# An ALiBi sliding-window attention and mixture-of-experts kernel: all heads' P.V in split bf16, queries in permuted groups, a new order of work

## The chip, the cores and the metric

One core of one Trainium2 chip runs the kernel. The metric is the device time of one execution in microseconds (us).

## The reference

```python
# q, k, v: (8 batches, 8 heads, 576 tokens, 64), fp32
scores = scale * np.matmul(q, k.transpose(0, 1, 3, 2))
scores = np.where((rel >= 0) & (rel < 128), scores + bias, -1e9)   # rel = query - key, bias = -slope[head] * rel
attn = softmax(scores)
x = (attn @ v), heads side by side: 4608 tokens x 512
y_dense = relu(x @ w1_dense) @ w2_dense
e = argmax(x @ w_gate)          # one of 8 experts for each token
y = y_dense + softmax(x @ w_gate)[e] * (relu(x @ w1[e]) @ w2[e])   # all weights 512 x 512
```

## The kernel before

The attention works in 16 units `u`: one batch and four heads (`hq`). A unit loads k and q as one transfer each (`load_qk`), 18 tokens to a partition, 32 partitions to a head. DVE turns them in blocks of 32x32 (`turn`, L345), and ACT rounds them to fp32r while it puts the tokens back in order, with a step of 18 elements in its output (`round_qk`, L352). Unit 0's query is rounded by DVE.

Each unit then has two rounds `r` (key tiles 0, 1 and 2, 3, 4). TensorE (PE) adds mask and bias with small products (`add_masks`, L536) and the scores (`scores`, L556); ACT takes the exponential for two heads at a time, `p` = 0 or 1 (`exps`, L567). P is fp32 and its bf16 upper half is read in place. `lows` (L579, DVE) writes P minus that half into the lower half as bf16, and `prep_v` (L365, POOL) does the same to V. `attend` sums P.V in PSUM as three bf16 products (high.high, high.low, low.high; L623) for a pair of key and query tile. With `OPT["whole"]` of 1 and `whole_to` of 12, units 0 to 11 take the last of their four heads as one fp32 product instead (L604): that head then needs no low parts, so `lows` of p = 1 has 512 columns there in place of 1024 and `prep_v` three heads in place of four. The last key tile has 64 rows. `norm` divides by the sums, `flip` and `keep` transpose for the gate.

After each batch the gate's logits choose an expert, tokens get slots in a DRAM table by expert (`count`, `slots`), and POOL scatters the rows (`send`, L846). Expert work goes in 43 blocks of 128 rows of one expert: 11 blocks after batch 4, 9 after batch 6, and 23 late ones after batch 8. A block is fetched through the SP queue, DVE copies its expert weights (`bring`, L1034), PE does layer 1 (L1044) and layer 2 (L1056) for the expert and for the dense part, ACT the ReLU, DVE the sum (L1070), POOL the scatter to the output (L1074). Early blocks take the ReLU in two halves (L1384) and have one buffer `yo` for the sum; late ones take it as one instruction over two banks (L1319) and keep sums in the six `p` buffers.

All of it is issued in an order made ahead by `Plan.order`: every part has an engine, a cost, a wanted time (`PACE` by unit, an offset and step from `PLACE`) and rooms (buffers, `ROOMS`). A list scheduler picks, on each engine, the part with the least wanted time among those that can start within `SLACK` of the first. The chip then runs each engine's list in that order. `OPT["flat"]` of 1 makes the set `FLAT` empty, so the functions for flat loads aren't used.

## Time and profile before

| | |
|---|---|
| time, median of 3 | 434.71 us (429.52 to 437.95) |
| profiled execution | 433.74 us, span 431.8 us |
| mean granted clock of TensorE | 0.887 |
| busy, share of the span | PE 86%, DVE 59%, ACT 54%, POOL 48% |

The span is from the first to the last instruction; what remains of the execution's time lies around it. PE and PEld are TensorE's matmuls and weight loads, DVE VectorE, ACT ScalarE, POOL GpSimd, SP SyncE, whose queue issues most loads.

### The profile page before, as it was taken

The numbers are of one execution on the slowest core, as the hardware profiler recorded it, in microseconds if no ns is written. First come the engines' busy times: TensorE is split into PE (matmuls) and PEld (weight loads), VectorE is DVE, ScalarE is ACT, GpSimd is POOL, SyncE is SP. The second block draws the span as 40 slices with busy tenths as digits, with TensorE's granted clock in tenths as the row PEclk, the third lists the DMA queues.
The fourth block names the chain that finished last, engine by engine and source line by source line (L and its number), as shares of the span: only waits on it lengthen the run. The fifth ranks groups of instructions, "written<-read, shape, count | busy, mean of one in ns | idle before, by whom it ended". The sixth has DMA issues, their size and how long they took to land.

```text
span 431.8 us, 12406 instructions
## 1 busy us (share of the span) xinstructions
PE 370.2 (86%) x5005; PEld 285.7 (66%) x5039; DVE 252.9 (59%) x438; ACT 233.1 (54%) x274; POOL 206.6 (48%) x265
## 2 busy tenths in 40 slices
PE   3499989897897977999798999779876999999993
PEld 0377877685685865787666776667654676767681
DVE  5576736748597578458969898563532243434331
ACT  5656655624667747547638996324332444444442
POOL 5060450508687818637743447657362242424241
PEclk9999967958586995569979999979989999999998
DMA  9979777951969986995436722133263433434330
GB/s 212 261 176 218 148 156 174 161 151 57 225 173 189 268 186 180 137 249 150 113 81 179 196 52 75 46 73 107 74 181 88 111 89 96 79 97 110 91 99 13
DMA packets 88808, 59.60 MB, mean 138 GB/s; under 512 B 70959, under 2 KB 81199, under 8 KB 88752
## 3 DMA queue, kind: packets, MB, share of 16 engines
q1 hardware_dynamic: 73872, 34.54, 33.3%
q0 software_dynamic: 14736, 23.68, 24.2%
q8 instruction: 40, 0.66, 0.6%
q10 hardware_dynamic: 144, 0.59, 0.5%
q14 instruction: 16, 0.13, 0.1%
HBM read 47.29 MB, written 17.13 MB: 149 GB/s over the span
## 4 chain that ended last, share of the span: by engine, by line
PE 43%; issue 18%; DVE 15%; POOL 12%; DMA 6%; ACT 3%; POOLq 1%; DVEq 0%; SPq 0%; ACTq 0%
PE ax L623 12%; POOL out_dram L1074 7%; PE ax L604 7%; PE sq L556 6%; PE misc L1044 5%; PE misc L1056 4%; DVE p L579 4%; DVE stg L345 3%; PE misc L683 3%; PE sq L536 2%; DMA rawq<-in_q_dram 2%; PE misc L716 2%; DVE xf L642 2%; DVE ws L1034 2%; POOL xs_dram L846 2%
## 5 line engine op out<-in xcount | busy, mean ns | idle before, releaser
L623 PE MATMUL ax<-vf,p 128*128 128x65 bf16 (+5 forms) x1404 | 84.7, 212 | 20.1 <-DVE p L579 13.3
L623 PEld LDWEIGHTS <-p 128*128 128x128 bf16 (+2 forms) x1404 | 72.4, 113 | 35.2 <-DVE p L579 14.7
L579 DVE TENSOR_TENSOR p<-p 128x1024 bf16<-128x1024 f32 x64 | 77.5, 1241 | 10.8 <-ACT p L567 10.8
L567 ACT ACTIVATE p<-sq 128x1024 f32<-128x1024 f32 x64 | 63.0, 1024 | 36.5 <-PE sq L556 35.9
L846 POOL DMA_INDIRECT xs_dram<-xrow,slot x40 | 45.7, 1141 | 32.1 <-issue 12.5
L664 POOL CAST xrow<-xf 128x512 bf16<-128x512 f32 x32 | 27.9, 876 | 46.1 <-DVE xf L642 45.9
L1056 PE MATMUL misc<-w_all,hT 128*128 (+1 forms) x138 | 41.9, 399 | 8.2 <-DVE yo L1070 5.4
L1074 POOL DMA_INDIRECT out_dram<-p,xm x23 | 24.5, 1065 | 51.0 <-DVE p L1070 51.0
L352 ACT CAST kT<-stg 128x1152 fp32r<-128x1152 f32 x16 | 37.7, 2356 | 18.2 <-DVE stg L345 18.2
L604 PE MATMUL ax<-vf,p 128*128 128x65 f32 (+2 forms) x216 | 46.7, 343 | 0.0
L1384 ACT ACTIVATE hT<-misc 128x512 bf16<-128x512 f32 x40 | 24.2, 607 | 39.1 <-PE misc L1044 39.1
L1074 POOL DMA_INDIRECT out_dram<-yo,xm x20 | 24.2, 1208 | 43.6 <-DVE yo L1070 34.9
L1044 PEld LDWEIGHTS <-w_all 128*128 128x128 bf16 x688 | 40.4, 98 | 5.2 <-issue 3.3
L604 PEld LDWEIGHTS ax<-vf,p 128*128 128x128 f32 (+2 forms) x216 | 37.7, 241 | 1.9
L352 ACT CAST qT<-stg 128x1152 fp32r<-128x1152 f32 x15 | 35.4, 2359 | 3.6 <-DVE mx L753 2.4
L365 POOL TENSOR_TENSOR vf<-vf 128x960 bf16<-128x960 f32 (+1 forms) x15 | 29.6, 1971 | 14.5 <-DMA vf<-in_v_dram 14.4
L556 PE MATMUL sq<-qT,kT 32*128 32x256 f32 (+2 forms) x640 | 32.8, 344 | 4.2 <-DVE qT L352 3.6
L1319 ACT ACTIVATE xT<-sq 128x1024 bf16<-128x1024 f32 x23 | 23.5, 1023 | 23.8 <-PE sq L1044 23.8
L556 PEld LDWEIGHTS sq<-qT,kT 32*128 32x128 f32 (+1 forms) x640 | 26.9, 235 | 11.7 <-issue 5.6
L1070 DVE TENSOR_TENSOR yo<-misc,ye 128x512 f32<-128x512 f32 x20 | 13.8, 688 | 33.0 <-DMA out_dram<-yo,xm 25.4
L641 DVE RECIPROCAL recip<-ax 128x8 f32<-128x8 f32 x32 | 6.6, 207 | 43.9 <-PE ax L604 40.6
L1034 DVE COPY ws<-w_all 128x2048 bf16 x20 | 24.2, 1208 | 12.6 <-PE misc L1044 11.3
(127 smaller groups left out, 601.9 us busy)
## 6 DMA issues: line engine op xcount, KB each, us to landing
rawk<-in_k_dram SPq DMA_DIRECT2D x16, 576.0 KB
rawq<-in_q_dram SPq DMA_DIRECT2D x15, 576.0 KB
vf<-in_v_dram SPq DMA_DIRECT2D x64, 128.0 KB
w_all<-in_moe_w_dram POOLq DMA_DIRECT2D x16, 512.0 KB, 8.1
xs_dram<-fill_x SPq DMA_DIRECT2D x8, 130.0 KB
vf<-in_v_dram SPq DMA_DIRECT2D x16, 64.0 KB
w_all<-in_moe_w_dense_dram POOLq DMA_DIRECT2D x2, 512.0 KB, 9.4
xTm<-xs_dram SPq DMA_TRANSPOSE x43
```

The source lines that it names most:

```text
L352: copy(out=d.rearrange("p c (x r) -> p c r x", r=R), in_=s.rearrange("p c (r x) -> p c r x", r=R),)
L365: eng.tensor_tensor(out=vb[:, :, hs, 0:D, 0], in0=vf[:, :, hs, 0:D], in1=vb[:, :, hs, 0:D, 1], op=ALU.subtract,)
L556: nc.tensor.matmul(out=sq[g // 2][:nk, g % 2, PCOL[kj] : PCOL[kj] + nq], lhsT=kT[r0 : r0 + n, c, kj * P : kj * P + nk], rhs=qT[r0 : r0 + n ...
L567: nc.scalar.activation(out=p32, in_=T[(f"sq{p}", u, r)], func=ACT.Exp, scale=SCALE)
L579: nc.vector.tensor_tensor(out=lo[:, 0:n], in0=T[("p", u, r, p)][:, 0:n], in1=hi[:, 0:n], op=ALU.subtract,)
L604: nc.tensor.matmul(out=ax[:rows, i, o0 : o0 + D + 1], lhsT=T[("p", u, 0 if kj < 2 else 1, p)][:ks, g % 2, c0 : c0 + rows], rhs=vfs[u % 3][ ...
L623: nc.tensor.matmul(out=ax[:rows, i, o0 : o0 + w], lhsT=lhs, rhs=rhs, start=(n == 1), stop=(n == 3 * len(kl)),)
L846: ins = nc.gpsimd.indirect_dma_start(out=xs_dram[:, :], out_offset=bass.IndirectOffsetOnAxis(ap=gst["slot", b][:rows, t : t + 1], axis=0), ...
L1034: nc.vector.tensor_copy(out=ws.unsqueeze(1), in_=w_all[:, bass.DynSlice(er, 1), 0, :, :])
L1044: nc.tensor.matmul(out=hp[:, c * P : c * P + P], lhsT=ws[:, kc, c * P : (c + 1) * P], rhs=xT[:, kc, :], start=(kc == 0), stop=(kc == 3),)
L1056: nc.tensor.matmul(out=y, lhsT=hT[:, c * P : c * P + P], rhs=w_all[:, E, 1, c, :] if dense else w_all[:, bass.DynSlice(er, 1), 1, c, :], s ...
L1074: ins = nc.gpsimd.indirect_dma_start(out=out[:, :], out_offset=bass.IndirectOffsetOnAxis(ap=T["xm", j][1].bitcast(I32)[:, 1:2], axis=0), i ...
```

## The change

The fp32 product goes: all heads of all units are three bf16 products, `lows` always has 1024 columns and `prep_v` four heads. The tail key tile is taken with 128 rows (rows 64 to 127 have masked P and zero V). The query is loaded by four transfers, one for a head, so that a partition holds pairs of tokens of each group of 64; after the turn its columns stand in a permuted order within each group, which the mask's iotas and the token numbers (`place_f`) follow, and the rounding becomes a plain copy. The key is turned in two instructions (one for each half of the 64 elements) with the two tokens of a pair side by side, and rounded in order of its output. Unit 0's query is rounded by ACT. Late blocks take the ReLU in two instructions, the first after the expert half. The planner's costs, `PACE` and all of `PLACE` are new, so every engine's list is ordered anew; the planner now holds one of the six `p` buffers until the constants that lie in it are read; unused code goes.

```diff
-OPT = {"flat": 1, "whole": 1, "whole_to": 12, "stages": [(4, 11), (6, 9)], "wsc": 11.0}
-PACE = [1.49, 14.89]
+OPT = {"stages": [(4, 11), (6, 9)], "wsc": 11.0}
+PACE = [11.15, 18.09]
...
-    "br0": (-17.98, 1.09), "br1": (-21.39, 11.49), "br2": (-17.07, 11.38), "bv": (35.71, 1.08),
...
+    "br0": (36.43, 5.54), "br1": (22.11, 2.82), "br2": (7.79, 11.87), "bv": (-18.67, 1.11),
...
-    def load_qk(u, nm, eng):
+    def load_k(u, eng):
         b, hq = divmod(u, HQ)
-        t = buf(("raw" + nm, u), [P, R, 2, 32], F32)
         eng.dma_start(
-            out=t.rearrange("p r c d -> p (r c d)"),
-            in_={"q": q, "k": k}[nm][b, 4 * hq : 4 * hq + 4].rearrange(
-                "h (p r) d -> (h p) (r d)", r=R
-            ),
-        )
+            out=buf(("rawk", u), [P, R, 2, 32], F32).rearrange("p r c d -> p (r c d)"),
+            in_=k[b, 4 * hq : 4 * hq + 4].rearrange("h (p r) d -> (h p) (r d)", r=R),
+        )
...
+    def load_q(u, h, eng):
         b, hq = divmod(u, HQ)
+        tok = ("rawq", u)
+        t = T[tok] if h else buf(tok, [P, R, 2, 32], F32)
+        eng.dma_start(
+            out=t[32 * h : 32 * h + 32].rearrange("p (g r) c d -> p g (r c d)", r=2),
+            in_=q[b, 4 * hq + h].rearrange("(g p r) d -> p g (r d)", p=32, r=2),
+        )
...
     def turn(u, nm):
-        s = buf(("stg", nm, u), [P, 2, S], F32)
-        nc.vector.transpose(
-            out=s.rearrange("p c (r x) -> p r c x", r=R), in_=T[("raw" + nm, u)]
-        )
-
-    def round_qk(u, nm, copy=nc.scalar.copy):
-        s = T[("stg", nm, u)]
-        d = buf((nm + "T", u), [P, 2, S], F32R)
-        copy(
-            out=d.rearrange("p c (x r) -> p c r x", r=R),
-            in_=s.rearrange("p c (r x) -> p c r x", r=R),
-        )
-
-    def halves(t):
-        h = t.bitcast(BF16)
-        return h
+        raw, s = T[("raw" + nm, u)], buf(("stg", nm, u), [P, 2, S], F32)
+        if nm == "q":
+            nc.vector.transpose(out=s.rearrange("p c (r x) -> p r c x", r=R), in_=raw)
+            return
+        for c in range(2):
+            nc.vector.transpose(
+                out=s[:, c].rearrange("p (r x e) -> p r e x", r=R // 2, e=2),
+                in_=raw[:, :, c].rearrange("p (r e) x -> p r e x", e=2),
+            )
+
+    def round_q(u):
+        nc.scalar.copy(out=buf(("qT", u), [P, 2, S], F32R), in_=T["stg", "q", u])
+
+    def round_k(u):
+        d = buf(("kT", u), [P, 2, S], F32R)
+        nc.scalar.copy(
+            out=d.rearrange("p c (x r e) -> p c x r e", r=R // 2, e=2),
+            in_=T["stg", "k", u].rearrange("p c (r x e) -> p c x r e", r=R // 2, e=2),
+        )
 
     def prep_v(u, eng=nc.gpsimd):
         vf = vfs[u % 3]
         vb = vf.bitcast(BF16).rearrange("p n h (d t) -> p n h d t", t=2)
-        hs = slice(0, 4 - WHOLE[u])
         eng.tensor_tensor(
-            out=vb[:, :, hs, 0:D, 0],
-            in0=vf[:, :, hs, 0:D],
-            in1=vb[:, :, hs, 0:D, 1],
+            out=vb[:, :, :, 0:D, 0],
+            in0=vf[:, :, :, 0:D],
+            in1=vb[:, :, :, 0:D, 1],
             op=ALU.subtract,
...
-    load_qk(0, "k", nc.sync)
-    load_qk(0, "q", nc.scalar)
+    load_k(0, nc.sync)
+    for h in range(4):
+        load_q(0, h, nc.scalar)
...
-            d_i[:, c0 : c0 + w], pattern=[[1, w]], base=base, channel_multiplier=-1
+            d_i[:, c0 : c0 + w],
+            pattern=[[64, w // 64], [1, 2], [2, 32]],
+            base=base,
+            channel_multiplier=-1,
...
+    place_i = consts.tile([P, 1], I32, name="place_i")
+    for i in range(4):
+        nc.gpsimd.iota(
+            place_i[32 * i : 32 * i + 32, :],
+            pattern=[[0, 1]],
+            base=64 * (i // 2) + i % 2,
+            channel_multiplier=2,
+        )
+    place_f = consts.tile([P, 1], F32, name="place_f")
+    nc.vector.tensor_copy(out=place_f, in_=place_i)
...
-    round_qk(0, "k")
+    round_k(0)
     turn(0, "q")
-    round_qk(0, "q", nc.vector.tensor_copy)
+    round_q(0)
...
     def lows(u, r, p):
         hi, lo = split(u, r, p)
-        n = min(2, max(0, 4 - WHOLE[u] - 2 * p))
-        if n:
-            nc.vector.tensor_tensor(
-                out=lo[:, 0:n], in0=T[("p", u, r, p)][:, 0:n], in1=hi[:, 0:n],
-                op=ALU.subtract,
-            )
+        nc.vector.tensor_tensor(
+            out=lo, in0=T[("p", u, r, p)], in1=hi, op=ALU.subtract
+        )
...
-                    ks = min(P, S - kj * P)
+                    ks = P
                     hi, lo = split(u, 0 if kj < 2 else 1, p)
                     c0 = PCOL[kj] + (0 if qi == kj else P)
-                    if g >= 4 - WHOLE[u]:
-                        n += 3
-                        nc.tensor.matmul(
-                            out=ax[:rows, i, o0 : o0 + D + 1],
-                            lhsT=T[("p", u, 0 if kj < 2 else 1, p)][
-                                :ks, g % 2, c0 : c0 + rows
-                            ],
-                            rhs=vfs[u % 3][:ks, kj, g, :],
-                            start=(n == 3),
-                            stop=(n == 3 * len(kl)),
-                        )
-                        continue
                     hi = hi[:ks, g % 2, c0 : c0 + rows]
                     lo = lo[:ks, g % 2, c0 : c0 + rows]
...
+    done("ints", take=[("p", "ints")])
     for i, f in enumerate((consts_a, consts_b, consts_c)):
-        add(("con", i), "DVE", (1.0, 1.3, 0.8)[i], f, 1.0, i)
+        add(("con", i), "DVE", (1.0, 1.3, 0.8)[i], f, 0.0, i, use=[("p", "ints")])
...
+            add(
+                ("ldk", u), "SP", 0.45, lambda u=u: load_k(u, nc.sync), u,
+                take=[("rawk", u)], move=1.9,
+            )
+            add(
+                ("tnk", u), "DVE", 1.31, lambda u=u: turn(u, "k"), u, take=[("stg", "k", u)],
+                use=[("rawk", u)],
+            )
+            add(
+                ("rnk", u), "ACT", 1.6, lambda u=u: round_k(u), u, take=[("kT", u)],
+                use=[("stg", "k", u)],
+            )
+            for h in range(4):
                 add(
+                    ("ldq", u, h), "SP", 0.42, lambda u=u, h=h: load_q(u, h, nc.sync), u, h,
+                    take=[] if h else [("rawq", u)], use=[("rawq", u)] if h else [], move=0.53,
+                )
+            add(
+                ("tnq", u), "DVE", 1.31, lambda u=u: turn(u, "q"), u,
+                after=[("ldq", u, h) for h in range(4)], take=[("stg", "q", u)],
+                use=[("rawq", u)],
+            )
+            add(
+                ("rnq", u), "ACT", 1.1, lambda u=u: round_q(u), u, take=[("qT", u)],
+                use=[("stg", "q", u)],
+            )
...
-            1.35 if u == 0 else 0.1 + 0.63 * (4 - WHOLE[u]),
+            1.35 if u == 0 else 2.3,
...
-                    ("lo", u, r, p), "DVE", (1.15, 0.6, 0.01)[nw],
+                    ("lo", u, r, p), "DVE", 1.25,
...
-                def re(j, sq=sq, ht=ht):
-                    t = buf(ht, [P, 2, BANK], F32).rearrange("p a x -> p (a x)")
-                    T["h", j] = t = t.bitcast(BF16)[:, 0 : 2 * BANK]
+                def re(j, d, sq=sq, ht=ht):
+                    if not d:
+                        t = buf(ht, [P, 2, BANK], F32).rearrange("p a x -> p (a x)")
+                        T["h", j] = t.bitcast(BF16)[:, 0 : 2 * BANK]
                     nc.scalar.activation(
-                        out=t.rearrange("p (a x) -> p a x", a=2),
-                        in_=T[sq],
+                        out=T["h", j][:, d * BANK : d * BANK + BANK],
+                        in_=T[sq][:, d, :],
                         func=ACT.Relu,
                     )
 
...
-                    "re", "ACT", 0.95, lambda j=j, f=re: f(j), after=[("l1d", j)],
+                    "re", "ACT", 0.5, lambda j=j, f=re: f(j, 0), after=[("l1e", j)],
                     use=[sq, ht],
                 )
                 one(
-                    "l2e", "PE", 0.87, lambda j=j, f=l2: f(j, False), after=[("re", j)],
+                    "rd", "ACT", 0.5, lambda j=j, f=re: f(j, 1), after=[("l1d", j), ("re", j)],
+                    use=[sq, ht],
+                )
+                one(
+                    "l2e", "PE", 0.93, lambda j=j, f=l2: f(j, False), after=[("re", j)],
                     take=yt[0:1] + [ot], use=[ht],
                 )
                 one(
-                    "l2d", "PE", 0.87, lambda j=j, f=l2: f(j, True), after=[("l2e", j)],
+                    "l2d", "PE", 0.87, lambda j=j, f=l2: f(j, True), after=[("l2e", j), ("rd", j)],
                     take=yt[1:2], use=[ht] + (yt if len(yt) == 1 else []),
                 )
                 one(
-                    "ye", "ACT", 0.5, lambda j=j, f=ye: f(j), after=[("l2e", j)],
+                    "ye", "ACT", 0.59, lambda j=j, f=ye: f(j), after=[("l2e", j)],
                     use=[ot, yt[0], ("xm", j)],
```

## Rows read from the trace of the kernel before

**Rows 1.** Busy time of PE over the span (share, instructions).
```profile
PE 370.2 (86%) x5005; PEld 285.7 (66%) x5039; DVE 252.9 (59%) x438; ACT 233.1 (54%) x274; POOL 206.6 (48%) x265
```
**Rows 2.** Busy time by stage; last three columns: granted clock, DMA share, GB/s.
```profile
core 0: us, PE busy (x) PEld busy (x) DVE busy (x) ACT busy (x) POOL busy (x), PEclk, DMA share, GB/s
0.00:20.00 20.00, 7.29 (x77) 3.42 (x77) 10.16 (x11) 11.59 (x13) 5.71 (x28) 1.00 1.03 237
20.00:220.00 200.00, 176.71 (x2471) 144.08 (x2474) 137.89 (x235) 117.52 (x123) 107.30 (x110) 0.79 0.77 172
220.00:304.00 84.00, 75.51 (x1259) 58.78 (x1272) 61.04 (x107) 51.42 (x68) 47.48 (x56) 0.95 0.38 101
345.00:425.00 80.00, 78.19 (x872) 56.98 (x882) 29.07 (x43) 36.53 (x44) 28.62 (x45) 1.00 0.37 91
```
**Rows 3.** Chain that ended last, 20 to 304 us, shares by line.
```profile
by line: PE ax L623 18.9%; PE ax L604 10.9%; PE sq L556 8.4%; PE misc L1044 6.7%; DVE p L579 6.1%; PE misc L1056 6.0%; PE misc L683 3.8%; issue 3.6%; DVE stg L345 3.5%; PE sq L536 3.3%; PE misc L716 3.0%; DVE xf L642 2.9%; DVE ws L1034 2.6%
```
**Rows 4.** L604 alone by stage: PE busy, PEld busy, clock, DMA.
```profile
20.00:220.00 200.00, 46.72 (x216) 37.65 (x216) 0.79 0.77 172
```
**Rows 5.** Timeline of PE: start, duration (us), line, shape, records.
```profile
62.09 1.10 PE L604 MATMUL ax<-vf,p 128*128 128x65 f32 x4
...
63.32 1.09 PE L604 MATMUL ax<-vf,p 128*128 128x65 f32 x4
...
75.61 2.10 PE L623 MATMUL ax<-vf,p 128*128 128x65 bf16 x42
77.55 0.63 PE L604 MATMUL ax<-vf,p 128*128 128x65 f32 x4
...
78.22 0.63 PE L604 MATMUL ax<-vf,p 128*128 128x65 f32 x4
...
106.11 2.70 PE L623 MATMUL ax<-vf,p 128*128 128x65 bf16 x36 [1.50 <-DVE xf L642]
...
108.75 1.11 PE L683 MATMUL misc<-ident_f,xf 128*128 128x128 f32 x4
```
**Rows 6.** Groups by line and shape: busy us, mean ns, idle before.
```profile
L579 DVE TENSOR_TENSOR p<-p 128x1024 bf16<-128x1024 f32 x40 | 59.4, 1488 | 10.8 <-ACT p L567 10.8
...
L352 ACT CAST kT<-stg 128x1152 fp32r<-128x1152 f32 x16 | 37.7, 2356 | 18.2 <-DVE stg L345 18.2
...
L352 ACT CAST qT<-stg 128x1152 fp32r<-128x1152 f32 x15 | 35.4, 2359 | 3.6 <-DVE mx L753 2.4 <-DVE stg L345 1.2
...
L1384 ACT ACTIVATE hT<-misc 128x512 bf16<-128x512 f32 x40 | 24.2, 607 | 39.1 <-PE misc L1044 39.1
L1034 DVE COPY ws<-w_all 128x2048 bf16 x20 | 24.2, 1208 | 12.6 <-PE misc L1044 11.3 <-DVE xrow L822 0.8 <-issue 0.3
...
L1319 ACT ACTIVATE xT<-sq 128x1024 bf16<-128x1024 f32 x23 | 23.5, 1023 | 23.8 <-PE sq L1044 23.8
...
L345 DVE STREAM_TRANSPOSE stg<-rawk 128x1152 f32<-128x1152 f32 x16 | 21.9, 1368 | 4.8 <-DMA rawk<-in_k_dram 4.8
...
L365 POOL TENSOR_TENSOR vf<-vf 128x960 bf16<-128x960 f32 x11 | 20.3, 1841 | 14.5 <-DMA vf<-in_v_dram 14.4
L579 DVE TENSOR_TENSOR p<-p 128x512 bf16<-128x512 f32 x24 | 19.9, 830 | 0.0
...
L1034 DVE COPY p<-w_all 128x2048 bf16 x23 | 15.5, 705 | 1.4 <-issue 1.1 <-DVE p L1034 0.2
```
**Rows 7.** Who waited for line L352 (us, times).
```profile
  PEld sq L556: 5.3, 3
```
**Rows 8.** Chain that ended last, in order of time: start, us.
```profile
9.49 8.50 DMA rawq<-in_q_dram
```
**Rows 9.** Timeline of DVE, sums of early blocks: first and last of eight.
```profile
308.82 0.69 DVE L1070 TENSOR_TENSOR yo<-misc,ye 128x512 f32<-128x512 f32 x1 [0.33 <-PE misc L1056]
...
345.73 0.69 DVE L1070 TENSOR_TENSOR yo<-misc,ye 128x512 f32<-128x512 f32 x1 [3.04 <-DMA out_dram<-yo,xm]
```
**Rows 10.** Busy time in windows of 3.4 us, columns as in rows 2.
```profile
83.20:86.60 3.40, 1.41 (x28) 0.88 (x28) 3.30 (x4) 2.86 (x3) 2.37 (x2) 1.00 1.23 250
...
90.00:93.40 3.40, 3.40 (x35) 2.84 (x39) 0.47 (x2) 1.11 (x3) 0.00 (x0) 0.50 0.87 249
```

111 lines of the change are left out of this document (21 added, 90 removed), and 35 rows, old and new, of the table PLACE.

## The prediction

> **What bounds the kernel now.** I read the page's busy times first: TensorE leads with 370.2 of 431.8 us, 61.6 idle [rows 1]. Then the span cut into stages [rows 2]. In the last one, 345 to 425, PE is busy 78.2 of 80 us at the full clock: 872 matmuls, at 40 a block 21.8 expert blocks, 3.67 us each. Nothing in the change takes a matmul from there. So whatever is gained comes ahead of it, above all in 20 to 220, where units 0 to 11 of the attention run: PE is busy 88%, DVE 69%, ACT 59%, POOL 54%, and the granted clock is 0.79, a mix of 2.4 and 1.2 GHz. The chain of waits over 20 to 304 says the same by line [rows 3]: products of P with V on top (18.9% at L623, 10.9% at L604), DVE's lows (L579) 6.1%, the turns (L345) 3.5%; no ACT line stands among its leaders. The end is set by PE's own list, with DVE the engine that it waits for most often.
>
> **P.V of the fourth head.** L604 is the fp32 product that goes: 216 records, 46.72 us busy, all of it in 20 to 220 [rows 4]. Two records are one product and a timeline row holds four, so 54 groups of two products. A row's duration holds the pipeline's tail, so I price by starts [rows 5], at the two levels of the clock, which show in the rows themselves (the same group lasts 0.63 in one place and 1.10 in the other). At 2.4 GHz the six bf16 products of head 2 and one L604 group take 78.22 - 77.55 = 0.67 us; at 1.2 GHz 63.32 - 62.09 = 1.23. After the change they are twelve bf16 products. 42 of these took 77.55 - 75.61 = 1.94 us (46 ns each) at the high level, 36 took 108.75 - 106.11 = 2.64 (73 ns) at the low one: 0.55 and 0.88 for twelve. So a group saves 0.12 or 0.35. Which level: the mean L604 group lasts 46.72 / 54 = 0.865, halfway between the rows' 0.63 and 1.10, so half of each: 54 x 0.235 = **-12.7**. I take it whole, because PE's list bounds this stage. Low end: only the share of L604 that lies in the chain counts, 10.9% of 284 = 31.0 of 46.7, which makes -8.4. High end: the rows' durations taken at face value (0.63 and 1.10 less six bf16 products, 0.28 and 0.44), 54 x 0.505 = 27, times that share, -18. The tail keys over 128 rows change no count; they go at nothing.
>
> **The lows.** Head 3 now needs its low part: 24 DVE subtractions grow from 512 to 1024 columns, 0.830 to 1.488 us [rows 6], 24 x 0.658 = 15.8 us more for DVE. Of L579's 79.3 us (59.4 and 19.9), 6.1% of 284 = 17.3 lie in the chain, 0.22. So **+3.5**, between 0 and 15.8. This speaks against the change most, as the P.V of both halves now waits for a long low.
>
> **The roundings on ACT.** Contiguous copies grow by (1023 - 607) / 512 = 0.81 ns a column [rows 6], so 1152 columns take 1.13 us. The query rounding becomes one: 15 x (2.36 - 1.13) = 18.5 us off ACT. For the key, in pairs, no row exists; it lies between 1.13 and 2.36, and with the middle, 1.74, 16 x 0.61 = 9.8 go. But PE waited only 5.3 us for these copies [rows 7], and 28.3 of the 73.1 us they last go, 39%: **-2.1** (0 to -5.3). Unit 0's query rounding moves from DVE to ACT behind the key's; the first scores then wait for both in one row, and what follows waits for unit 1's load anyway [rows 8], so it is nothing; without that cover 1.13.
>
> **The key turn in two.** 1.368 us of DVE [rows 6] becomes two instructions of 576 columns with a step in the output. With time by columns, only one more start is added: by the two lows, 0.830 - 0.658 = 0.17. High end: the step halves the rate, as it does for the strided copy, 16 x 1.37 = 22. L345 is 43.7 us, 9.9 of it (3.5% of 284) in the chain, 0.23: from 0.6 to 5, and I take **+0.6**, nearest to the row of the same instruction.
>
> **The query load.** Four DMAs of 512-byte pieces for one of 4608-byte pieces, and three more issues on SP ahead of the value loads and fetches of the same queue. After the start the loads run ahead of their use. At the start they don't: the DMA engines are full in 0 to 20 [rows 2] and the chain sits 8.50 us on unit 1's query [rows 8]. No row has such pieces; between 0 and half of that wait again (4.3) I take **+1.0**, an estimate near the low end, because the bytes are the same.
>
> **POOL.** Three heads of value preparation take 1.841 us [rows 6], four would by proportion take 2.45, 11 x 0.61 = 6.7 us more, on an engine 54% busy; hidden, and 6.7 if not. One row does speak against it: the same copy of 2048 bf16 columns takes DVE 1.208 us on average while POOL prepares and scatters, and 0.705 later [rows 6]; DVE is slowed by something that runs beside it. The Trainium skill (SBUF — State Buffer, Who interferes with whom) says that a DVE instruction with two SBUF inputs shares a read port with GpSimd's reads, and that the later of the two is blocked outright. The lows have two such inputs and the preparation reads, so by that rule the 6.7 us also stretch lows, 6.7 x 0.22 = 1.5, and the sum would be 425.1.
>
> **ReLU split.** Two halves cost ACT 2 x 607 - 1023 = 191 ns more in each of 23 blocks, under an ACT that is busy 36.5 of 80 us there. PE is full, so it gains only at the last block: **-0.4**. The new iotas, placement constants and the query waits of the start lie under the loads.
>
> **The order.** Whole queues are re-sorted; no row prices that, and I put it at 0. What it can move shows in one place: between 308.82 and 345.73 the sums of early blocks come 36.9 / 7 = 5.27 us apart [rows 9], because each waits until the store of the one before has landed, against 3.67 later. Seven intervals x 1.6 = 11.2 us to win, or, with more early blocks left over, to lose.
>
> **Sum.** -12.7 + 3.5 - 2.1 + 0.6 + 1.0 - 0.4 = -10.1. The profiled execution took 433.74 (span 431.8 and 1.94 around it), 1 us under the median of 434.71. 433.74 - 10.1 = 423.6: **424 us**. A measurement of this kernel can tell about 2% from no change, that is under 426.0 or over 443.4.
>
> **Rival 1, a better fit (406).** P.V saves its high end (-5.3 more) and the new order interleaves the early blocks (-11.2): 407, and with one us off the query load 406. For it: both sizes are in the rows. Against: the order's gain is only room, no evidence.
>
> **Rival 2, DVE takes over (436).** All 15.8 us of lows lie on the path in place of 3.5: 423.6 + 12.3 = 435.9. For it: DVE's work in 20 to 220 rises from 137.9 to about 155, 78% of the stage, for an engine that waits in order for ACT and PE. Against: in 220 to 304, where all heads run in this very form, DVE is 73% busy and PE 90% [rows 2].
>
> **Rival 3, the clock (447, slower).** In 20 to 220 a pause of PE is followed by the lower level: at 83.2 PE is busy 1.41 of 3.40 us, and at 90.0 it is busy throughout at 0.50 [rows 10]. Take the fp32 work away and add to DVE's, and PE pauses more often. Now 42% of that stage is at 1.2 GHz ((1 - 0.79) / 0.5). With bf16 products 73 / 46 = 1.59 times as long there, PE's 176.7 us are 149.2 at 2.4 GHz, 142.7 after the change (54 x 0.12 less). At a share s of 1.2 GHz they take 142.7 / (1 - 0.371 s): from s = 0.52 nothing is saved, and s = 0.65 makes 188.0, 11.3 more, at 88% busy 12.8 of time: 446.5. Against: 220 to 304 has this form at 0.95, though expert matmuls fill it. The Trainium skill (TensorE: Matmul & The Clock Gate, HAM oscillation) has it that idle between bursts puts the clock back down and the next burst starts cold; the rows at 83.2 and 90.0 agree, and by that rule less matmul work under the same waits is this rival.
>
> That the change doesn't do what it says (a key rounding in pairs that stays at 2.36, a query load that hurts) lies inside the bounds above: at most +0.8 and +3.3.
>
> **How the numbers follow.** Forecast (414 to 432) 0.50, of it 0.35 under 426.0; rival 1 0.16; rival 2 0.20; rival 3 0.14. Faster 0.35 + 0.16 = 0.51, the same 0.15 + 0.20 = 0.35, slower 0.14. The range runs from 404, just under rival 1, to 439, rival 2 with a key turn near its high end (+3); rival 3 and the far ends of rival 1 stay out.
>
> **What would show it.** L604 gone, L623 at 1728 matmuls and PE near 164 us busy in the stretch of units 0 to 11; 64 lows near 1.49 us; query copies near 1.13, key copies between 1.13 and 2.36; the last stage still 3.67 us a block. The forecast is wrong if waits of PE for DVE grow by ten us or more (rival 2), if the granted clock of that stretch falls under 0.74 (s = 0.52), or if the early blocks' spacing of 5.27 us is gone or has spread (the order).

## The result, and the profile after

The changed kernel takes 415.47 us (median of 4, 412.67 to 419.04) against 432.53 for the kernel before on the same chip (429.52 to 437.95): ratio 0.9585, interval 0.9491 to 0.9679. Ratios, here and below, leave out runs over 1.5% above the quickest of the same kernel, so they are not quotients of the medians. Forecast were 424 us and a move of -10; the move was -17. Run again later beside other kernels it took 419.40 against 430.54, ratio 0.9829 (0.971 to 0.9947); the two intervals don't overlap, so its size is known to some 2.5%. The profiled execution took 416.41 us, span 414.6.

Busy times and stages after, in the columns of [rows 1, 2]:

```profile
PE 322.8 (78%) x5147; PEld 246.5 (59%) x5147; DVE 269.4 (65%) x454; ACT 203.3 (49%) x298; POOL 226.0 (55%) x269
```
```profile
20.00:220.00 200.00, 144.80 (x2780) 117.50 (x2778) 165.46 (x262) 103.61 (x136) 127.99 (x113) 0.87 0.94 182
220.00:304.00 84.00, 75.91 (x1260) 57.61 (x1245) 62.02 (x132) 43.67 (x70) 55.55 (x67) 1.00 0.50 118
```

TensorE lost 370.2 - 322.8 = 47.4 us of busy time, the span only 431.8 - 414.6 = 17.2: the rest became idle time (61.6 to 91.8 us). Between 20 and 220 us 2780 matmuls take 144.8 us where 2471 took 176.7; the granted clock is 0.87 there in place of 0.79, and the DMA engines are 94% busy in place of 77%. The stretch doesn't hold the same work in both: its last attention unit, 11, ends at 219.39 us before and at 204.74 after.

Groups by line, answering to [rows 4, 6] (busy us, mean ns, idle before):

```profile
L555 DVE TENSOR_TENSOR p<-p 128x1024 bf16<-128x1024 f32 x64 | 101.2, 1609 | 10.6 <-ACT p L545 9.0 <-issue 1.6
L586 PE MATMUL ax<-vf,p 128*128 128x65 bf16 (+3 forms) x1728 | 80.1, 208 | 11.1 <-DVE p L555 9.7 <-DVE xf L605 0.6 <-issue 0.3
...
L313 DVE STREAM_TRANSPOSE stg<-rawk 128x576 f32<-128x576 f32 x32 | 23.0, 759 | 14.2 <-DMA rawk<-in_k_dram 14.2
L323 ACT CAST kT<-stg 128x1152 fp32r<-128x1152 f32 x16 | 19.5, 1221 | 13.9 <-DVE stg L313 13.9
L319 ACT CAST qT<-stg 128x1152 fp32r<-128x1152 f32 x16 | 18.5, 1158 | 8.6 <-DVE stg L310 6.1 <-DVE recip L604 2.4
```

The fp32 products are gone and 1728 bf16 products remain; query copies last 1.158 us, and the key copies in pairs 1.221, almost as little. One group doesn't fit the forecast: P.V as a whole was 84.7 us of bf16 and 46.7 of fp32, and is now 80.1 us with 324 more bf16 matmuls, each shorter (208 ns against 212).

Start of the profiled execution, load queues (SPq, ACTq) and what waits for them:

```profile
0.80 5.08 ACTq L281 DMA_DIRECT2D rawq<-in_q_dram  x4
5.91 1.28 ACT L464 ACT_TABLE_LOAD   x1 [5.91 <-DMA rawk<-in_k_dram]
12.96 1.83 SPq L281 DMA_DIRECT2D rawq<-in_q_dram  x4
14.84 3.25 SPq L291 DMA_DIRECT2D vf<-in_v_dram  x4
18.14 1.03 SPq L272 DMA_DIRECT2D rawk<-in_k_dram  x1
23.92 1.44 DVE L313 STREAM_TRANSPOSE stg<-rawk 128x576 f32<-128x576 f32 x2 [9.33 <-DMA rawk<-in_k_dram]
```

The four issues of unit 0's query hold ScalarE's queue for 5.08 us, and in the new order unit 1's query and values go out ahead of its key, whose turn waits 9.33 us. The end of a unit can be read from its last normalisation (the start of the xft row in VectorE's timeline): unit 0 ends at 44.67 us (before 35.22), unit 7 at 142.20 (146.68), unit 15 at 282.45 (298.86). The late blocks then run at two in 356.64 - 349.60 = 7.04 us:

```profile
349.60 0.69 DVE L1033 TENSOR_TENSOR p<-misc,p 128x512 f32<-128x512 f32 x1 [2.75 <-ACT p L1030]
...
356.64 0.69 DVE L1033 TENSOR_TENSOR p<-misc,p 128x512 f32<-128x512 f32 x1 [2.76 <-ACT p L1030]
```

That is 3.52 a block, near the 3.67 of the forecast. So about 10 us are lost at the start and some 26 won in units 1 to 15.

### The profile page after: what moved, and what is told of

It reads as the page before. It is cut to its first block, busy times and chain, and to the rows that moved or that the text cites. A ratio compares the mean times of both kernels' runs of the same rounds, so it can differ in the third digit from the quotient of the medians.

```text
span 414.6 us, 12784 instructions
## 1 busy us (share of the span) xinstructions
PE 322.8 (78%) x5147; PEld 246.5 (59%) x5147; DVE 269.4 (65%) x454; ACT 203.3 (49%) x298; POOL 226.0 (55%) x269
## 4 chain that ended last, share of the span: by engine, by line
PE 26%; DVE 25%; issue 21%; POOL 12%; DMA 10%; ACT 3%; SPq 2%; POOLq 1%; DVEq 0%; ACTq 0%
DVE p L555 11%; PE ax L586 10%; POOL out_dram L1037 8%; DMA out_dram<-yo,xm 5%; PE sq L534 4%; PE misc L1007 4%; DVE xf L605 3%; PE misc L1019 3%; DVE stg L310 3%; PE misc L646 3%; DMA vf<-in_v_dram 2%; DVE stg L313 2%; POOL xs_dram L809 2%; ACT p L545 1%; DMA rawq<-in_q_dram 1%
## 5 line engine op out<-in xcount | busy, mean ns | idle before, releaser
L555 DVE TENSOR_TENSOR p<-p 128x1024 bf16<-128x1024 f32 x64 | 101.2, 1609 | 10.6 <-ACT p L545 9.0
L586 PE MATMUL ax<-vf,p 128*128 128x65 bf16 (+3 forms) x1728 | 80.1, 208 | 11.1 <-DVE p L555 9.7
L586 PEld LDWEIGHTS <-p 128*128 128x128 bf16 (+1 forms) x1728 | 73.6, 110 | 19.7 <-DVE p L555 10.3
L545 ACT ACTIVATE p<-sq 128x1024 f32<-128x1024 f32 x64 | 63.2, 1022 | 31.9 <-PE sq L534 31.3
L809 POOL DMA_INDIRECT xs_dram<-xrow,slot x40 | 47.4, 1186 | 32.0 <-POOL xrow L806 9.3
L627 POOL CAST xrow<-xf 128x512 bf16<-128x512 f32 x32 | 35.7, 1117 | 32.8 <-DVE xf L605 32.7
L331 POOL TENSOR_TENSOR vf<-vf 128x1280 bf16<-128x1280 f32 x15 | 38.8, 2592 | 22.5 <-DMA vf<-in_v_dram 21.6
L1037 POOL DMA_INDIRECT out_dram<-yo,xm x20 | 24.7, 1236 | 33.3 <-DVE yo L1033 25.0
L646 PE MATMUL misc<-ident_f,xf 128*128 128x128 f32 x128 | 24.3, 320 | 21.4 <-DVE xf L605 15.1
L534 PE MATMUL sq<-qT,kT 32*128 32x256 f32 (+2 forms) x640 | 29.5, 314 | 10.9 <-ACT qT L319 10.0
L1277 ACT ACTIVATE xT<-sq 128x512 bf16<-128x512 f32 x46 | 25.0, 594 | 25.9 <-PE sq L1007 22.8
L655 ACT COPY xT<-misc 128x512 f32<-128x512 f32 x32 | 18.8, 587 | 34.0 <-PE misc L646 34.0
L313 DVE STREAM_TRANSPOSE stg<-rawk 128x576 f32<-128x576 f32 x32 | 23.0, 759 | 14.2 <-DMA rawk<-in_k_dram 14.2
L1019 PEld LDWEIGHTS <-xT 128*128 128x128 bf16 x184 | 17.5, 98 | 23.9 <-ACT xT L1277 3.4
L517 PE MATMUL sq<-mask,ident 32*32 32x512 bf16 x512 | 20.4, 418 | 9.1 <-ACT p L545 7.2
```

The costliest lines, as they stand in the source:

```text
L313: nc.vector.transpose(out=s[:, c].rearrange("p (r x e) -> p r e x", r=R // 2, e=2), in_=raw[:, :, c].rearrange("p (r e) x -> p r e x", e=2),)
L331: eng.tensor_tensor(out=vb[:, :, :, 0:D, 0], in0=vf[:, :, :, 0:D], in1=vb[:, :, :, 0:D, 1], op=ALU.subtract,)
L534: nc.tensor.matmul(out=sq[g // 2][:nk, g % 2, PCOL[kj] : PCOL[kj] + nq], lhsT=kT[r0 : r0 + n, c, kj * P : kj * P + nk], rhs=qT[r0 : r0 + n ...
L545: nc.scalar.activation(out=p32, in_=T[(f"sq{p}", u, r)], func=ACT.Exp, scale=SCALE)
L555: nc.vector.tensor_tensor(out=lo, in0=T[("p", u, r, p)], in1=hi, op=ALU.subtract)
L586: nc.tensor.matmul(out=ax[:rows, i, o0 : o0 + w], lhsT=lhs, rhs=rhs, start=(n == 1), stop=(n == 3 * len(kl)),)
```

## The experiments

The kernels ran in five groups, each on one chip beside the kernel before; medians are compared within a group where possible, because the kernel before itself stood between 430.3 and 435.7 us. "Copies" stands for the new loads, turns and roundings of query and key, "tail 128 rows" for the tail key tile taken with 128 rows. The kernels that combine the parts of the change:

| kernel | order | P.V bf16 | copies | tail 128 rows | ReLU split | median us | before, same group |
|---|---|---|---|---|---|---|---|
| e1_pv | old | yes | | | | 421.18 | 433.81 |
| e2_copies | old | | yes | | | 432.25 | 433.81 |
| e3_both | old | yes | yes | yes | | 411.36 | 433.81 |
| e4_fp32_back | new | | yes | yes | yes | 419.99 | 433.81 |
| e8_copies_back | new | yes | | yes | yes | 420.21 | 430.77 |
| e9_order_alone | new | | | yes | yes | 423.44 | 430.77 |
| e11_old_order | old | yes | yes | yes | yes | 407.27 | 430.54 |
| e13_changed_again | new | yes | yes | yes | yes | 419.40 | 430.54 |
| e14_tail_alone | old | | | yes | | 406.42 | 435.71 |
| e15_pv_tail | old | yes | | yes | | 405.46 | 435.71 |
| e16_pv_copies | old | yes | yes | | | 421.23 | 435.71 |
| e17_changed_tail64 | new | yes | yes | | yes | 422.28 | 435.71 |
| e18_order_only | new | | | | yes | 438.42 | 430.27 |
| e19_pv_tail_relu | old | yes | | yes | yes | 407.68 | 430.27 |

**Products alone (e1_pv).** The planner still sees the old costs, so the order stays.

```diff
+    PLANNED, WHOLE = WHOLE, [0] * (2 * B)
...
-            1.35 if u == 0 else 0.1 + 0.63 * (4 - WHOLE[u]),
+            1.35 if u == 0 else 0.1 + 0.63 * (4 - PLANNED[u]),
...
```

> The order of the kernel before, unchanged; only head 3 of units 0 to 11 goes over to three bf16 products, with its lows and its value preparation. Theory A (the fp32 products kept TensorE at 1.2 GHz for longer, which the sum didn't price): in 20 to 220 the granted clock rises from 0.79 to 0.85 or more, stretches at 0.50 last 3 to 8 us instead of 10 to 31, and the time falls by 10 to 18 us. Theory B (as in the prediction, the saving is that of the products alone): -12.7 + 3.5 = -9 us at a clock of 0.79. Theory C (the new order and the cheaper copies made the gain, DVE takes back what PE saves): within 3 us of before.

421.18 us, 12.6 under before by the medians; its four runs are 411.78, 420.17, 422.19 and 422.94, so the gain is known only to lie between 11 and 22. The mean clock of its runs is 0.898, of before 0.891, and from 20 to 220 us it is 0.80 for 0.79: theory A's rise to 0.85 didn't come. In this order the fp32 products don't hold the clock down.

**Copies alone (e2_copies).** Loads, turns, roundings and query groups of the change in the old order.

```diff
+        if nm == "k":
+            load_k(u, eng)
+        else:
+            for h in range(4):
+                load_q(u, h, eng)
...
+        (round_q if nm == "q" else round_k)(u)
...
```

> The order of the kernel before, unchanged; only the loads, turns and roundings of query and key are the new ones (four query loads, key turned in pairs, permuted queries, unit 0's query rounded by ACT); the fp32 product stays. Theories A and B: small, -4 to +4 us (28 us less on ACT, of which PE waited for 5; the start later by some us, since the first query lands later). Theory C: -8 us or more. Query copies 1.16 us, key copies 1.22, key turns 2 x 0.72.

Ratio 1.0032 (0.9963 to 1.0102): no difference of more than 1%, so theory C falls. Unit 0 ends at 39.16 us, 4 later than before, and that is won back.

**Both together (e3_both).** The two edits above and, as I copied the changed product loop, the tail keys over 128 rows.

```diff
-                    ks = min(P, S - kj * P)
+                    ks = P
```

> All edits to P.V, tail keys, loads, turns and roundings, in the order of the kernel before; late ReLU in one instruction. What then remains to the changed kernel (-17 us) is the new order and the split ReLU. Theory A: about the sum of the two runs alone, -10 to -18 us, clock in 20 to 220 at 0.85 or more; the new order is worth no more than 5 us either way. Theory C: no more than -8, the order brings the rest.

411.36 us, ratio 0.9537 (0.9481 to 0.9592). I took the 10 us beyond e1_pv for the copies. That was wrong: the kernel differs from e1_pv in the tail keys too.

**fp32 product back in the changed kernel (e4_fp32_back).**

```diff
+                    if g >= 4 - WHOLE[u]:
+                        n += 3
+                        nc.tensor.matmul(
+                            out=ax[:rows, i, o0 : o0 + D + 1],
+                            lhsT=T[("p", u, 0 if kj < 2 else 1, p)][
...
```

> The changed kernel in its own order, with the fp32 product of head 3 in units 0 to 11 put back (short lows, three heads of value preparation). Theory A: clock in 20 to 220 back from 0.87 to 0.80 or less, long stretches at 0.50 again, time up by 10 to 18 us although DVE has 16 to 20 us less to do. Theory B: up by 9. Theory C: within 4 us of the changed kernel, or below it.

419.99 us, ratio 0.9701 (0.9628 to 0.9775). That lies between the two measurements of the changed kernel (0.9585 and 0.9829): in its order the products are worth 5 us at most, perhaps nothing, and not the 9 of theory B. The granted clock from 20 to 220 us did go back from 0.87 to 0.80, as theory A has it, but not the 10 to 18 us: here the fp32 products come with the lower clock, in the old order (e1_pv) they don't.

**One bf16 product for head 3 (e5_one_product).** Old order, both corrections left out.

```diff
-                            lhsT=T[("p", u, 0 if kj < 2 else 1, p)][
-                                :ks, g % 2, c0 : c0 + rows
-                            ],
-                            rhs=vfs[u % 3][:ks, kj, g, :],
+                            lhsT=hi[:ks, g % 2, c0 : c0 + rows],
+                            rhs=vb[:ks, kj, g, 0 : D + 1, 1],
```

> The order of the kernel before; head 3 of units 0 to 11 takes one bf16 product of the upper halves in place of the fp32 product, so its two corrections are left out, and the lows stay short: TensorE has less to do than with three products (216 matmuls, some 10 to 16 us) and DVE nothing more than before. If it is the kind of work that holds the clock down (fp32 products), the granted clock rises clearly above the 0.89 of before, to 0.92 or more, and the time falls by 20 us. If the clock follows TensorE's pauses alone, less work under the same waits leaves it at 0.89 or lowers it, and the time falls by 10 to 15.

405.65 us, ratio 0.9499 (0.9326 to 0.9673), 25 under before; by the medians the three-product form of e1_pv keeps half of that. The mean clock is 0.887, in the kernel before beside it 0.882: less work did not raise it to the 0.92 of the first case, and the time fell all the same.

**Unit 1's key first (e7_key_first).** The changed kernel with one load pulled to the head of the order.

```diff
-    for _, part in plan.order(free, SLACK):
+    todo = [part for _, part in plan.order(free, SLACK)]
+    first = next(p for p in todo if p.key == ("ldk", 1))
+    todo.remove(first)
+    for part in [first] + todo:
```

> The changed kernel with one move: on SP, unit 1's key load is issued ahead of unit 1's query and value loads instead of behind them. If the new order lost its 9 us at the start there (the key turn of unit 1 waited 9.3 us for this load), unit 0 ends at about 38 us instead of 44.7 and the kernel takes 409 to 412. If the start is bound by the bytes of all loads in flight, or is made up for later, nothing changes (414 to 417).

The second case: 416.92 us (414.62 to 420.52). Unit 0 ends at 42.37 and unit 1 at 53.22, 2 to 3 us earlier, far from the 38 hoped for, and nothing of it arrives at the end.

**Old copies in the new order (e8_copies_back), and without bf16 products too (e9_order_alone).** The functions load_qk, turn and round_qk of before, called from the new parts; both keep the tail keys over 128 rows.

```diff
...
-        nc.scalar.copy(out=buf(("qT", u), [P, 2, S], F32R), in_=T["stg", "q", u])
+        round_qk(u, "q")
...
```

> The changed kernel with the old loads, turns and roundings of query and key (2.36 us each on ACT), everything else and the order as changed. In the old order the three bf16 products alone gave about 12 us and with the new copies 22, so the copies are worth 10 there although they gave nothing alone. If ACT's roundings are the next bound once the fp32 product is gone, this one takes 420 to 426 and its granted clock falls from 0.93 to about 0.90. If the new order makes do without them, 413 to 418.

> The changed kernel's order and split ReLU with the old P.V and the old copies: the order alone. Undone one at a time, the products cost 5 us in this order against 21 in the old one, so the new order copes better with fp32 products. If that is the order's own worth, this takes 422 to 427; if the order only works with the cheaper copies, 430 to 440.

420.21 us, ratio 0.9845 (0.9715 to 0.9975), and 423.44, ratio 0.991 (0.9857 to 0.9963). The first is level with the changed kernel run again (0.9829), and its clock, 0.911 to 0.926, didn't fall to 0.90. I read the second as a new order that gains 7 by itself; its tail keys make that reading void (e18_order_only).

**GpSimd's preparation (e10_prep_three).** e1_pv with three heads subtracted again.

```diff
-        hs = slice(0, 4 - WHOLE[u])
+        hs = slice(0, 3 if 0 < u < 12 else 4)
...
-                        (hi, vv[:, 0:D, 0], D),
+                        (hi, vb[:ks, kj, 2 if g == 3 and 0 < u < 12 else g, 0:D, 0], D),
```

> The bf16 products in the order of the kernel before (421.2 us), with GpSimd's subtraction of the values' high half made for three heads again in units 1 to 11, as in the kernel before; the product of head 3 takes head 2's low half there, so that this head's correction is not computed rightly, while TensorE and VectorE do the same work as in that kernel. Theory P (the subtraction, one head longer, stands in the way of VectorE's small operations between units 4 and 6, and TensorE pauses behind them): most of the 9.8 us between the products alone (421.2) and products with the new copies (411.4) comes back, 411 to 414, and units 4 to 6 take about 31 us in place of 40. Theory S (what the new copies give is ScalarE's time, which the cheap products uncover): 419 to 422, units 4 to 6 still near 40.

413.45 us (411.51 to 414.44), ratio 0.9675 (0.9555 to 0.9796). The time fits theory P, the place doesn't: units 5 and 6 still take 124.98 - 85.58 = 39.4 us (e1_pv 40.3, e3_both 30.2), and the small two-input operation on `oh`, which theory P blames, averages 0.753 us here and 0.785 in the quicker e11_old_order. The 8 us under e1_pv's median may be that kernel's spread, whose runs reach down to 411.78, or a gain from the shorter subtraction at another place; that isn't settled. What theory P was made to explain, the 9.8 us between e1_pv and e3_both, the tail keys below explain, so I dropped it.

**Order undone (e11_old_order), roundings twice (e12_round_twice), the change again (e13_changed_again).** The first is e3_both with the split ReLU, the second e3_both with each rounding repeated.

```diff
-                    nc.scalar.activation(
-                        out=t.rearrange("p (a x) -> p a x", a=2),
-                        in_=T[sq],
-                        func=ACT.Relu,
-                    )
+                    for d in range(2):
+                        nc.scalar.activation(
+                            out=t[:, d * BANK : d * BANK + BANK],
+                            in_=T[sq][:, d, :],
+                            func=ACT.Relu,
+                        )
```
```diff
+        if 0 < u < 12 and nm == "q":
+            nc.scalar.copy(out=T["qT", u], in_=T["stg", "q", u])
...
```

> All edits of the change except the order and the planner's numbers: bf16 products, new copies, tail keys over 128 rows, and the ReLU of the late blocks split in two, its two halves one after the other behind the second layer-1 product. Theory O (the new order is worth less than nothing once the other edits are in): 410 to 412, and 3 to 5 us under the changed kernel in the same call. Rival (the products and copies in the old order came out low by chance, or the split ReLU needs the new order): 414 to 416, level with the changed kernel. If the two halves behind one another cost ScalarE 0.15 us a block in the late stage, at most 23 x 0.15 = 3.5 us more.

> Products and new copies in the old order (411.4 us), with ScalarE's rounding of query and key made twice in units 1 to 11, the second time over the first: 11 x (1.16 + 1.22) = 26 us more ScalarE, which puts its busy time between 20 and 220 us back from 106 to about 130, where the old copies had it (128). Theory S (the worth of the new copies is ScalarE's time): 419 to 422, as with the old copies. Theory P (GpSimd against VectorE's small operations): 410 to 414, since neither of them has more work.

> The changed kernel unaltered, beside the three others on the same chip. 413 to 417 us by every theory; what counts is its distance to the kernel with all other edits in the old order: 3 to 5 us if the new order costs time on top of them, under 2 if not.

407.27, 411.16 and 419.40 us. Repeating the roundings puts ScalarE's busy time between 20 and 220 us from 105.7 to 130.9; the kernel takes 411.16, ratio 0.9634 (0.9521 to 0.9747), where e3_both without the repeats has 411.36 and 0.9537. No cost is clear of the noise, the 419 of theory S is far off, and it falls. The same edits take 12.1 us longer in the new order than in the old one, not 3 to 5. With both theories gone I compared P.V itself, first e1_pv, then e3_both:

```profile
L624 PE MATMUL ax<-vf,p 128*128 128x65 bf16 (+3 forms) x1728 | 97.5, 214 | 21.2 <-DVE p L580 11.7 <-DVE xf L643 8.7 <-issue 0.2
```
```profile
L660 PE MATMUL ax<-vf,p 128*128 128x65 bf16 (+3 forms) x1728 | 82.8, 209 | 29.5 <-DVE p L616 17.4 <-DVE xf L679 11.5 <-DVE xft L690 0.5
```

The same 1728 products, 14.7 us apart. The two kernels differ in the copies and in the tail keys, and the next runs part them.

**Tail keys (e14_tail_alone, e15_pv_tail, e16_pv_copies, e17_changed_tail64).** The one line above in the kernel before, and with the products; products with copies without it; the changed kernel with it undone.

> The kernel before with one edit: the tail keys' products run over 128 rows in place of 64, as in the changed kernel. Theory T (products over 64 rows cost TensorE time beyond their own length, which the prediction put at nothing): the two kernels with the new copies that run them over 128 rows show the same 1728 products in 82.8 and 83.8 us of TensorE against 97.5 and 97.8 where they run over 64, so 12 to 15 us less of TensorE, some of it behind waits: 420 to 426. Rival C (the copies made that difference): 430 to 434, as before.

> The bf16 products in the old order with old copies, and the tail keys over 128 rows. Theory T: 408 to 413, all that the products with copies and tail keys together gave (411.4), and P.V near 83 us of TensorE. Rival C: 419 to 422, as the products alone (421.2), P.V near 97.

> The bf16 products in the old order with the new loads, turns and roundings, the tail keys over 64 rows as in the kernel before. Theory T: 418 to 423, no better than the products alone (421.2). Rival C: 409 to 413.

> The changed kernel with the tail keys over 64 rows again, nothing else. Theory T: 8 to 13 us over the changed kernel, 424 to 430. Rival C: level with it, 415 to 420.

406.42 us, ratio 0.9309 (0.9236 to 0.9382): one line gives 29 us, more than the whole change. That is also 14 under the 420 to 426 of theory T, which counted TensorE's busy time alone. With the products 405.46, ratio 0.9239 (0.9154 to 0.9325). Products and copies without it 421.23, ratio 0.9651 (0.9576 to 0.9726), as the products alone. Theory T holds in kind, rival C falls. The changed kernel without it takes 422.28, 3 to 7 over its two medians with it and under the 424 to 430 expected; its four runs go from 415.21 to 425.09, the quickest level with the changed kernel, so there the edit's worth is open between nothing and 7.

**The order by itself (e18_order_only), and the split beside tail and products (e19_pv_tail_relu).** The first is e9_order_alone with the line below, the second e15_pv_tail with the split of e11_old_order.

```diff
-                    ks = P
+                    ks = min(P, S - kj * P)
```

> The new order and the split ReLU alone: fp32 products, old loads, turns and roundings, tail keys over 64 rows. With the tail keys over 128 rows this order took 423.4 us, where the old order takes 406.4. If the order by itself is worth nothing, as predicted: 428 to 436, and all of the 17 us between those two is time that the old order can give back and the new one can't. If the new order costs by itself: 438 to 446. If it gains by itself, as I first read from the 423.4: 421 to 426.

> Old order, old copies, bf16 products, tail keys over 128 rows and the split ReLU. Against the same without the ReLU's split (405.5) it prices the split, against the same with the new copies (407.3) it prices the copies. If the split gives what it seemed to give beside the new copies (411.2 to 407.3): 401 to 403. If it is worth the 0.4 us of the prediction: 404 to 406. Either way under the changed kernel (415.5 to 419.4).

438.42 us, ratio 1.0177 (1.0065 to 1.029): the new order, with the split, costs 8 by itself. Against e9_order_alone the tail keys are worth 11 (by the ratios) to 15 us (by the medians) in the new order too, as long as the fp32 products stand. 407.68 us, ratio 0.9457 (0.9386 to 0.9528), where the same without the split took 405.46, ratio 0.9239, in another group: no gain from the split is to be seen, nor, against e11_old_order's 407.27, from the copies. The quickest version is one of e14_tail_alone and e15_pv_tail, which aren't told apart; both beat the change.

## Why the prediction was right in sign and wrong in size

**The step that failed.** Two terms that the sum put at nothing were the large ones: the tail keys, -29 us by themselves, and the order, +8 to +17 by what stands beside it. The first is the step that made the forecast too small: "The tail keys over 128 rows change no count; they go at nothing." No count changes, but the time does. The timeline of the kernel before shows it (start, duration); the left-out line is the one at 78.22 of [rows 5]:

```profile
78.02 0.36 PE L623 MATMUL ax<-vf,p 128*128 128x65 bf16 x6
...
78.78 0.49 PE L623 MATMUL ax<-vf,p 128*64 128x65 bf16 x6
79.20 0.58 PE L604 MATMUL ax<-vf,p 128*64 128x65 f32 x4
79.72 0.43 PE L536 MATMUL sq<-mask,ident 32*32 32x512 bf16 x16
```

and the same place in e14_tail_alone:

```profile
63.25 1.76 PE L623 MATMUL ax<-vf,p 128*128 128x65 bf16 x42
64.85 0.63 PE L604 MATMUL ax<-vf,p 128*128 128x65 f32 x4
65.32 0.36 PE L623 MATMUL ax<-vf,p 128*128 128x65 bf16 x6
65.51 0.63 PE L604 MATMUL ax<-vf,p 128*128 128x65 f32 x4
66.08 0.38 PE L623 MATMUL ax<-vf,p 128*64 128x65 bf16 x6
66.30 0.42 PE L604 MATMUL ax<-vf,p 128*64 128x65 f32 x4
66.65 0.43 PE L536 MATMUL sq<-mask,ident 32*32 32x512 bf16 x16
```

Go by starts. Six products over 128 rows take 78.22 - 78.02 = 0.20 us; the six of the tail queries, three of them over 64 rows, 79.20 - 78.78 = 0.42, though they have half the weight columns. Over 128 rows throughout they take 66.30 - 66.08 = 0.22. The fp32 group goes from 0.52 to 0.35. So half a unit (two heads) loses 0.37 us where TensorE passes from 128 rows to 64 and back for each head, and 32 halves some 12 us, an estimate at the higher level of the clock.

The starts of single records in the two traces show that the price is that of the passage, not of the 64 rows. At 2.4 GHz a bf16 product over 64 rows starts 123 ns after one over 128 rows with as many weight columns (median of 41), and one over 128 rows 120 ns after one over 64 (17); in e14_tail_alone, over 128 rows throughout, the next starts after 34 (226). Behind a passage three products over 64 rows start 54 and 35 ns apart, three over 128 rows with as many columns 54 and 36 (medians of 41 each in the kernel before). So a passage costs some 0.09 us, and the 64 rows by themselves nothing. The one from 128 weight columns to the 64 of the tail queries costs as much and stays: 126 ns in both kernels (17 and 16). The Trainium skill (TensorEngine Tiling (Array Packing), Tiling Modes) says that a change of the tiling mode drains TensorE; the rows agree with that.

The price also stood, unseen, in the row by which I priced bf16 products. The 42 products that took 77.55 - 75.61 = 1.94 us are the row of 63.25 above, which takes 64.85 - 63.25 = 1.60: 38 ns a product, not 46, because six of the 42 were over 64 rows. Six over 128 rows take 0.20 us, 33 ns each. So the fp32 products' replacement was priced too dear, while the tail keys went at nothing.

**Where the other 17 of the 29 us come from.** P.V by line in e14_tail_alone, with a line that the edit doesn't touch:

```profile
L623 PE MATMUL ax<-vf,p 128*128 128x65 bf16 (+3 forms) x1404 | 72.4, 206 | 18.0 <-DVE p L579 11.5 <-DVE xf L642 6.4
...
L604 PE MATMUL ax<-vf,p 128*128 128x65 f32 (+1 forms) x216 | 37.8, 299 | 0.0
L556 PE MATMUL sq<-qT,kT 32*128 32x256 f32 (+2 forms) x640 | 29.3, 315 | 4.9 <-DVE qT L352 3.7 <-ACT qT L352 1.2
```

TensorE's busy time falls by 370.2 - 336.9 = 33.3 us: 12.3 in L623 (84.7 before), 8.9 in L604 (46.7), and 12.1 in lines that run the same instructions, such as L556 (32.8 before). The last part, and what P.V loses beyond the 12 us of passages, go with the granted clock of 20 to 220 us, 0.86 in place of 0.79: cut into single microseconds, 51 of these 200 are at 1.2 GHz throughout where 79 were. Why fewer passages leave TensorE longer at 2.4 GHz isn't settled. In the new order the same line raises the clock from 0.79 to 0.84 beside the fp32 products (e18_order_only to e9_order_alone) and leaves it at 0.87 beside the bf16 ones (e17_changed_tail64 to the changed kernel), where the gain, too, is 7 us or less.

**P.V and lows (-12.7 + 3.5).** Alone, e1_pv measured -12.6 by its median: near the -9.2 of the sum, but by two errors against each other. TensorE's busy time fell by 370.2 - 352.4 = 17.8 us, more than the 12.7, and more of it was lost to waits than the 3.5. Beside the tail keys P.V is worth 1 us (406.42 to 405.46), which isn't told from nothing. "I take it whole, because PE's list bounds this stage" fails there. Stage 20 to 220 of e14_tail_alone and of e15_pv_tail:

```profile
20.00:220.00 200.00, 172.22 (x2946) 141.78 (x2955) 156.89 (x263) 139.98 (x149) 120.83 (x123) 0.86 0.87 194
```
```profile
20.00:220.00 200.00, 158.25 (x2952) 126.79 (x2960) 166.48 (x255) 135.49 (x144) 138.17 (x120) 0.84 0.85 189
```

TensorE works 14 us less and the attention gets no further (unit 11 ends at 194.08 and at 195.99 us), so all of it turns into waiting. Its waits there in e14_tail_alone, largest first (total, times, longest), then in e15_pv_tail:

```profile
PE ax L623 <- DVE p L579: 11.5, 7, 5.0
PE ax L623 <- DVE xf L642: 6.4, 7, 2.0
PE sq L536 <- ACT p L567: 3.4, 7, 1.1
...
PE misc L683 <- DVE xf L642: 0.7, 1, 0.7
```
```profile
PE ax L624 <- DVE p L580: 12.8, 8, 4.3
PE ax L624 <- DVE xf L643: 8.7, 8, 2.6
PE sq L537 <- ACT p L568: 4.7, 9, 1.1
PE misc L684 <- DVE xf L643: 4.4, 1, 4.4
PE misc L777 <- DVE oh L765: 4.2, 2, 3.9
```

These are mostly waits for VectorE, whose work rises by 9.6 us in the stage: rival 2's mechanism, decided not by the lows alone but by TensorE having become short enough. The sum was additive; once the tail keys are mended the two terms are not.

**Order (0).** It costs in every pair, by the medians: 8 us alone (before to e18_order_only), 12 with all else in (e11_old_order to e13_changed_again), and across groups 17 (e14_tail_alone to e9_order_alone) and 15 (e15_pv_tail to e8_copies_back). The 8 is with roundings for which this order was not made; TensorE's largest wait from 20 to 220 us is there for the query's:

```profile
PE sq L535 <- ACT qT L317: 14.9, 8, 4.0
```

In the kernel before that wait is 0.5 us, in the changed kernel 5.9. In the pair with all else in, unit 0 ends 4.7 us later (43.98 to 39.28), unit 3 9.7 (85.79 to 76.11), unit 11 5.1, unit 13 15.0, unit 15 8.0, the last sum 10.9 (409.15 to 398.29). So the first four units lose nearly as much as the whole, and what follows wins and loses on top of it. Waits of TensorE from 20 to 86 us, first in the changed kernel run again, then in the old order:

```profile
PE misc L646 <- DVE xf L605: 9.0, 4, 5.0
PE ax L586 <- DVE p L555: 7.9, 1, 7.9
PE sq L534 <- ACT qT L319: 3.0, 2, 1.7
```
```profile
PE ax L660 <- DVE p L616: 7.3, 3, 4.8
PE ax L660 <- DVE xf L679: 6.5, 4, 2.8
PE misc L720 <- DVE xf L679: 4.5, 1, 4.5
PE sq L573 <- ACT p L604: 0.9, 2, 0.5
```

The first come to 24.5 us with three smaller rows that are left out, the second to 19.2: 5 of the 10 us. Which move costs them stays open; e7_key_first shows that it isn't unit 1's key load alone.

**Roundings (-2.1), key turn (+0.6), query load (+1.0).** Together -0.5 forecast; e2_copies measured no difference, and can't tell one of under some 3 us. The -2.1 was a misreading even so: of the 5.3 us of [rows 7], 4.1 are one wait for unit 0's key copy, over at 10.86 us, so only 1.2 are left for all later copies. The sizes: query copy 1.158 us for 1.13; key copy 1.221 for the middle of 1.74; key turn 2 x 0.759 = 1.52 for 1.368 + 0.17; the first unit's end 4 us later, the far end of the 4.3 given for the query load, but only at the start.

**ReLU split (-0.4).** Below what these comparisons show.

**Rival 3, the clock.** It went the other way, 0.79 to 0.87 from 20 to 220 us. Rival 1's 406 was reached, by neither of its reasons, in e14_tail_alone. The sum as measured: -29 for the tail keys, -1 for the products beside them, 0 for the copies, +12 for the order, -18, where the change measured -17 and -11. That is one path from the one kernel to the other. Order first, by the ratios, gives other sizes: +8, then -12 for the tail keys (e9_order_alone), -3 for the products (e8_copies_back), -1 for the copies (e13_changed_again). That the time lies in the prediction's range is luck: a gain and a loss that it both put at nothing partly cancel.

**Signs named.** TensorE at 164 us in the stretch of units 0 to 11: 144.8 from 20 to 220, with work beyond unit 11 in it, the first sign that a term was missing. Lows at 1.49 us: 1.609 in the new order, 1.490 in e1_pv. The early blocks' spacing of 5.27 us: (324.77 - 287.26) / 7 = 5.36 for the last eight, so the order moved nothing there. The sign for rival 2, ten us more of waits for VectorE, did come. From 20 to 220 us these waits sum to 22.8 us before and 41.9 after; the largest of each:

```profile
PE ax L623 <- DVE p L579: 11.8, 6, 4.3
PE ax L623 <- DVE xf L642: 6.4, 6, 2.0
```
```profile
PE misc L646 <- DVE xf L605: 15.1, 8, 5.0
PE ax L586 <- DVE p L555: 9.7, 3, 8.1
PE misc L665 <- DVE xft L616: 7.4, 4, 3.7
```

The time fell none the less, because TensorE had been spared more than it waited: its busy time in the stretch fell by 176.7 - 144.8 = 31.9 us.

## What to carry to other kernels

When an edit changes the shape of an instruction, read that instruction's own row start to start in the trace of before, even if the count stays: here the price of the passage to 64 rows and back stood in it, and inside the mean of a row used to price something else. Undo or do each part alone before naming a cause, and make the difference of two kernels one edit; my combined kernel carried a second one, and two theories were tested for nothing. A gain on one engine's list lasts until the next engine is as late, so terms worked out one by one don't add, and an order planned anew has to be run against the old one with the same instructions.

## What was unexpected of the hardware

Products over 64 rows between products over 128 cost more than the full rows: 0.42 us against 0.22 for the same six, some 0.09 us for each passage. The passages to the tail queries' 64 weight columns and back remain, two for half a unit: at most 32 x 2 x 0.09 = 6 us, an estimate from the same records; no run here removes them. Rounding the key in pairs runs near the contiguous rate (1.221 and 1.158 us, against 2.356 with the old step). VectorE's operation on `oh`, 128 x 40, takes 0.20 us in seven of its eight times in e11_old_order and once 4.87, until GpSimd's subtraction on `vf` beside it ends (start, duration):

```profile
143.44 4.87 DVE L801 TENSOR_TENSOR oh<-em8x,e 128x40 bf16<-128x40 f32 x1
145.88 2.38 POOL L389 TENSOR_TENSOR vf<-vf 128x1280 bf16<-128x1280 f32 x1
```

In the changed kernel run again it is once 3.52 us, in its first profile never over 0.28, so the averages (0.785, 0.616 and 0.211 us) are each set by one instruction or none; what such a stall costs at the end was not separated.
